# A new order list for an attention and feed-forward kernel: the same 1349 pieces of work, arranged anew

## The chip, the cores and the metric

The kernel runs on one core of a Trainium2 chip. The core's engines work side by side, each through its own queue of instructions, in order: TensorE (PE; PEld for its weight loads), VectorE (DVE), ScalarE (ACT), GpSimd (POOL) and SyncE (SP), which issues most of the DMAs. What is measured is the device time of one execution in microseconds. The kernel before took 220.15 us, the median of three runs (219.94 to 220.78). One execution of it was profiled, and all rows of a profile come from that one.

## The reference

The result is `x + A(xn) + B(xn)` with `xn = layernorm(x)` over 2048 rows of 512 columns.

A is attention with 32 heads of 16 columns over four segments of 512 rows, with a memory that is handed from segment to segment:

```python
p = _softmax(qs @ ks.T * scale + mask)
a_dot = p @ vs
pq, pk = phi(qs), phi(ks)            # phi(t) = t + 1 where t > 0, else exp(t)
a_mem = (pq @ M) / (pq @ z + 1e-06)
o = g * a_mem + (1.0 - g) * a_dot
M = M + pk.T @ vs;  z = z + pk.sum()
```

and then `o @ wo`. B is `silu(xn @ w1) @ w2` with 1792 hidden columns. Weights and x are bf16.

## The kernel before, in words

Rows come in 16 tiles of 128; four tiles are a segment. Nothing is scheduled by a planner at build time: the text `ORDER` (from line 16) lists 1349 words, one for each piece of work, and a loop at the end of the kernel calls the pieces in exactly that order. Each engine gets its instructions in the order in which the words name them, so the list fixes every engine's queue. What words on different engines do in time is settled by the semaphores alone.

A word is a name and its numbers. The ones that matter here:

- `xs`, `xc`+`xd` (statistics of a tile on VectorE, lines 286 and 289), `xq`+`xi` (root on ScalarE and reciprocal, for tiles 0 to 3; `xg` does four tiles on GpSimd for the others), `Nv t` (the norm of tile t on VectorE, line 315).
- `X` (transpose on TensorE, line 845, first segment) with its copies `Xa` on ScalarE and `Xv` on VectorE (line 851); `XD` (transpose by DMA on SP's queue, the later segments).
- `k s.dt.part`, `q`, `v`, `h`: projections, in four parts each for segments 0 and 1 and in two for the others (lines 336 and 338). `kv`, `qv`, `vv` copy the result out of PSUM on VectorE, `ka`, `qa`, `va` on ScalarE (lines 376, 399, 406). `kp` makes the masked keys on GpSimd. `ha` is the tanh on ScalarE (line 492), `hv` the product that completes silu on VectorE (line 497).
- `S n`: a score of 4 heads' blocks, 72 of them, one 4-bank PSUM tile, and behind it the exponential on ScalarE (`Pb`, line 730) and the causal selects on GpSimd (line 744). The list is written with a new line at each `S`; such a line is called a stage.
- `E n`, `O n`: the weighing of the values by the exponentials (line 791), `Ev`, `Ea`, `Ov` their copies out (lines 821, 828). The copies also start small DMAs that gather the softmax sums (`zraw`, line 813). `Om` merges the odd halves.
- `fp`, `fa`, `fv`, `gp`, `ga`, `gv`: phi of the keys and queries; `t` and `m`, `mv`, `mw`: the memory update. `s`, `sv`, `r`, `w`, and in the last segment `R`, `W`: reciprocals of the sums; `z`, `d`: two DMAs each that spread them over the partitions (line 577); `zv`, `dv`, `n`, `nv`: their products and the sum into `oT` (lines 589, 599, 608).
- `o s.j.i`, `oc`, `od`, `oh`: products of the output, whole, half and quarter columns wide. `xl` loads the residual rows, `st` and `sh` add and store.
- `bmask`, `odd`, `omask`, `kind`, `gate`: small constants. `busy` is idle TensorE work at the start.

All results of TensorE but the scores share four PSUM banks (the pool `pp`): a projection, a weighing or an output tile takes a bank with its first product, and the bank is free when the word that copies it out (`kv`, `hv`, `Ev`, `st` and the like) is done. A score needs the score tile free, that is, the exponential of the score before.

A product runs whole (128 x 128 weights) or, between a weighing and the next score, as four column tiles of 32 (`narrow`); the list sets which by what stands ahead of it.

The loads at the start are issued ahead of the list and aren't in it: x tiles 0 and 2 and then wv, wk, wq, x tiles 4 to 7, w1 and the rest of x on SP's queue, x tiles 1 and 3 on ScalarE's.

Of the kernel before, what the change touches and what calls it, by code (L numbers as in the profile page):

```python
# [25 lines left out]
S6 fa0.3 k1.2.0 k1.2.1 k1.2.2 h0.5.0 h0.5.1 h0.5.2 q1.1.0 h0.5.3 ha0.5 k1.2.3 kv1.2 q1.1.1 q1.1.2 hv0.5
S8 h0.7.0 q1.1.3 qv1.1 h0.6.0 h0.6.1 h0.6.2 h0.6.3 ha0.6 fv0.3 E1 Ev1 k1.0.0
S9 hv0.6 h0.7.1 h0.7.2 h0.7.3 Om0 ha0.7 k1.0.1 k1.0.2 kp1.2 q1.0.0 q1.0.1 q1.0.2 fp0.1 Nv9 XD9 xs12 k1.0.3 kv1.0 kp1.0
S10 h0.8.0 hv0.7 h0.8.1 h0.8.2 h0.8.3 ha0.8 h0.9.0 h0.9.1 q1.0.3 t0.3 Nv10 XD10 h0.9.2 h0.9.3 qv1.0
S13 hv0.8 O1 Ov1 xs15 v1.0.0 v1.0.1 v1.0.2 ha0.9 v1.0.3 vv1.0 h0.10.0 h0.10.1 bmask  # L30
S12 k1.1.0 k1.1.1 k1.1.2 t0.2 k1.1.3 kv1.1 h0.10.2 h0.10.3 ha0.10 hv0.9 h1.0.0 Om1 h1.0.1 h1.0.2
S15 h1.10.0 h1.10.1 h1.10.2 hv0.10 kp1.1 xl0.2 h1.0.3 ha1.0 Nv11 XD11 E2 Ev2 O2 Ov2
S17 h1.10.3 k1.3.0 hv1.0 k1.3.1 k1.3.2 k1.3.3 kv1.3 fp1.3 h0.12.0 h0.12.1 xs14 m0.2 mv0.2 ha1.10 h0.12.2
S21 fv0.1 q1.3.0 q1.3.1 q1.3.2 q1.3.3 qv1.3 h1.3.0 hv1.10 gp1.1 h0.12.3 ha0.12 t0.1 h1.3.1 h1.3.2 t0.0 h1.3.3
S14 hv0.12 k2.2.0 h0.11.0 h0.11.1 k2.2.1 h0.11.2 h0.11.3 xl0.0 h0.13.0 ha1.3
S16 ha0.11 h0.13.1 h0.13.2 kp1.3 h0.13.3 xs13 kv2.2 hv1.3 ha0.13 q2.1.0 q2.1.1 qv2.1 E3
S19 Ev3 h1.11.0 h1.11.1 h1.11.2 h1.11.3 hv0.11 O3 hv0.13 fa1.3 k2.1.0 mw0.2 k2.1.1 Ov3 kv2.1 Om2
S24 h1.8.0 h1.8.1 h1.8.2 h1.8.3 m0.0 mv0.0 q2.3.0 q2.3.1 qv2.3 ha1.8 hv1.8
S18 v2.1.0 v2.1.1 vv2.1 ga1.0 k2.0.0 o0.2.7 oc0.2.5.0 ha1.11 sv0 r0.1 o0.2.4 k2.0.1 kv2.0 xg12.4
S22 fv1.3 v2.2.0 v2.2.1 vv2.2 o0.2.1 ga1.1 gp1.2 o0.2.6 o0.0.3 o0.0.13 od0.2.11.1 hv1.11 r0.2 o0.0.10  # L40
S20 o0.2.0 oc0.0.2.0 r0.3 lw1 o0.2.2 od0.0.0.2 oc0.2.10.1 h1.1.0 h1.1.1 h1.1.2 h1.1.3 kp2.1 E4 r0.0 od0.0.0.1 ha1.1 gate w0 gv1.1 kp2.0 z0.1
S28 o0.0.6 hv1.1 z0.2 o0.0.8 z0.3 o0.0.11 o0.0.5 Ev4 oc0.0.7.1 Om3 z0.0 o0.2.8 o0.0.12 ga1.2 O4 Ov4
S26 q2.0.0 q2.0.1 h1.7.0 h1.7.1 h1.7.2 h1.7.3 gv1.2 ha1.7 qv2.0 oc0.2.10.0 od0.0.0.3 oc0.0.2.1
S23 fp1.2 od0.2.11.3 h1.4.0 hv1.7 h1.4.1 h1.4.2 Nv14 o0.2.12 h1.4.3 ha1.4 od0.2.11.0 oc0.0.7.0 zv0.3 h1.9.0 o0.2.13 h1.9.1
S25 h1.9.2 h1.9.3 ha1.9 Nv12 XD12 o0.2.3 oc0.2.5.1 gp1.0 zv0.2 o0.2.16 o0.0.16 hv1.4 zv0.0 XD14 zv0.1 E5 o0.0.17 Ev5 hv1.9
S29 fa1.2 o0.2.17 o0.2.14 k2.3.0 gv1.0 k2.3.1 kv2.3 h1.2.0 h1.2.1 h1.2.2
S27 o0.0.9 mw0.0 O5 o0.2.15 Ov5 o0.2.9 Nv13 fp1.0 XD13 h1.2.3 ha1.2 od0.2.11.2 fv1.2 st0.2 t1.2 o0.0.14 o0.0.15
# [6 lines left out]
S41 o0.1.7 Ev7 o0.3.12 o0.1.1 hv1.5 O7 v2.3.0 mw1.2 fa1.1 Ov7 v2.3.1 vv2.3 fv1.1 t1.1
S37 o0.3.5 q3.3.0 q3.3.1 Om7 qv3.3 od0.1.8.1 s1 o0.1.5 sv1 r1.2 o0.1.10 oc0.1.9.1 st0.1 r1.0 od0.3.3.2 ga2.3 kp2.2
S36 k3.1.0 k3.1.1 q3.1.0 q3.1.1 qv3.1 r1.3 r1.1 w1 d1.2 z1.1 z1.2 ka3.1 o0.3.4
S40 h1.6.0 h1.6.1 h1.6.2 h1.6.3 fp2.3 h2.8.0 h2.8.1 ha1.6 o0.3.7
S43 oc0.3.0.0 o0.3.6 od0.3.3.0 hv1.6 od0.3.3.1 m1.0 mv1.0 oc0.3.2.0 od0.3.3.3 o0.3.15 st0.3 o1.2.8 ha2.8 o1.2.7 hv2.8 fv2.0 E8 Ev8 gp2.3
S38 o1.2.13 fa2.2 v3.0.0 v3.0.1 Om6 k3.0.0 od1.2.1.1 k3.0.1
# [6 lines left out]
S46 oc1.0.10.1 gv2.1 h2.12.0 z1.0 o1.0.5 h2.12.1 O9 Ov9 o1.0.8 ha2.12 hv2.12 t2.3
S49 o1.0.9 o1.0.17 h2.5.0 h2.5.1 kp3.0 ha2.5 n1.1 nv1.1 o1.2.17 fp2.1 oc1.0.10.0 o1.0.12
S53 o1.0.2 hv2.5 oc1.0.7.0 fa2.1 v3.1.0 v3.1.1 vv3.1 o1.0.15 xl2.0 E10 Ev10
S51 o1.2.12 n1.0 od1.0.1.2 xl1.3 od1.2.1.0 h2.4.0 zv1.0 h2.4.1 nv1.0 kp3.1 ha2.4 fv2.1 t2.1 gp2.0 o1.2.15 o1.0.3 hv2.4 o1.0.11
S50 o1.2.14 o1.2.16 st1.2 Om9 O10 Ov10 od1.0.1.1 h2.2.0 h2.2.1 ha2.2 hv2.2 o1.0.14 o1.1.9 od1.1.6.0  # L70
S52 Om10 o1.3.8 oc1.3.3.0 od1.1.6.3 o1.1.2 od1.0.1.0 st1.0 o1.1.15 od1.3.9.1 h2.9.0 h2.9.1 ha2.9 o1.3.15 hv2.9 gv2.2
S56 k3.3.0 k3.3.1 kv3.3 ga2.0 o1.1.17 oc1.1.7.0 xl1.1 E11 Ev11 oc1.3.3.1 oc1.1.10.1 gv2.0
S61 o1.3.7 o1.3.2 ga3.0 o1.1.16 O11 o1.1.13 m2.0 oc1.1.10.0 o1.1.11 o1.3.17 Ov11 od1.3.9.2
S54 mv2.0 od1.1.6.2 m2.2 o1.1.4 mv2.2 mw2.2 s2 sv2 o1.3.5 r2.3 Om11 fill h2.10.0 h2.10.1 ha2.10 hv2.10 gp3.0 o1.3.14
S55 o1.1.12 gv3.0 r2.1 r2.0 o1.3.6 oc1.1.7.1 o1.1.14 o1.3.13 r2.2 w2 o1.3.16 d2.0 h2.13.0 h2.13.1 ga3.1 o1.1.0 ha2.13 hv2.13
S58 h2.3.0 h2.3.1 o1.3.1 o1.1.5 o1.1.8 o1.3.12 od1.3.9.0 o1.3.0 ha2.3 hv2.3
# [866 lines left out]
```

## Time and profile before

| | before |
|---|---|
| median of three runs | 220.15 us |
| the profiled execution | 219.96 us |
| its span, first to last instruction | 218.2 us |
| TensorE busy | 210.9 us (97%) |
| ScalarE busy | 184.1 us (84%) |
| VectorE busy | 181.3 us (83%) |
| GpSimd busy | 127.4 us (58%) |
| exponentials (line 730) | 72, mean 1.878 us |

The profiled execution's 219.96 us is its span and 1.76 us around it. A row of a timeline gives the start in us from the span's beginning, the duration, the engine, the line of the program, the operation, what it writes and reads, a count, and in brackets how long the engine had been idle and for what. Matmuls overlap, so a row's duration is longer than the distance to the next one.

### The profile page before, as it was taken

The page shows a single profiled execution, that of the slowest core. Times are in us where ns is not written, and L with a number is a line of the kernel's source. Part 1 is how long each engine was busy: PE and PEld are TensorE (multiplying, and loading weights), DVE is VectorE, ACT ScalarE, POOL GpSimd, SP SyncE. Part 2 cuts the span into 40 slices and gives each one's busy share as a digit, 9 for nine tenths or more (in the row PEclk, how much of TensorE's full clock was granted, in tenths as well). Part 3 has the DMA queues.
Part 4 walks back from the last instruction along what each step waited for, and adds up shares of the span by engine and source line. Part 5 has one row for each costly group of instructions (what it writes and reads, how often), then busy time and mean ns, then how long its engine had stood idle before and what let it go on. Part 6 is the DMA issues. An engine that isn't in the chain of part 4 may idle for free.

```text
span 218.2 us, 9267 instructions
## 1 busy us (share of the span) xinstructions
PE 210.9 (97%) x3982; PEld 116.1 (53%) x4006; DVE 181.3 (83%) x370; ACT 184.1 (84%) x173; POOL 127.4 (58%) x203
## 2 busy tenths in 40 slices
...
DMA packets 33273, 19.60 MB, mean 90 GB/s; under 512 B 14672, under 2 KB 33232, under 8 KB 33232
## 3 DMA queue, kind: packets, MB, share of 16 engines
...
q14 instruction: 10, 0.08, 0.1%
HBM read 9.96 MB, written 2.10 MB: 55 GB/s over the span
## 4 chain that ended last, share of the span: by engine, by line
PE 92%; DMA 3%; ACT 2%; issue 1%; SPq 1%; DVE 0%
PE ps L336 26%; PE psO L338 17%; PE ps L338 16%; PE psS L724 11%; PE psO L336 9%; PE psV L791 8%; PE psS L338 4%; DMA wk_sb<-in_A_wk_dram 3%; ACT Pb L730 2%; PE psM L452 1%; SPq L169 0%; SPq L158 0%; PE ps L509 0%; ACT th L492 0%; DVE o_half L668 0%
## 5 line engine op out<-in xcount | busy, mean ns | idle before, releaser
L730 ACT ACTIVATE Pb<-psS 128x2048 bf16<-128x2048 f32 x72 | 135.2, 1878 | 4.7 <-PE psS L724 2.4
L744 POOL TENSOR_SCALAR_AFFINE_SELECT Pb<-Pb 128x512 bf16<-128x512 bf16 (+2 forms) x88 | 62.3, 718 | 22.4 <-ACT Pb L730 19.6
L497 DVE SCALAR_TENSOR_TENSOR hT<-th,ps 128x512 bf16<-128x512 bf16 x56 | 38.0, 682 | 10.1 <-ACT th L492 9.4
L744 POOL TENSOR_SCALAR_AFFINE_SELECT lows<-Pb 64x512 bf16<-64x512 bf16 (+1 forms) x40 | 24.3, 607 | 32.0 <-ACT Pb L730 24.9
L338 PE MATMUL psO<-w_sb,hT 128*32 128x512 bf16 (+2 forms) x696 | 41.4, 321 | 0.0
L336 PE MATMUL ps<-xnT,w_sb 128*128 128x512 bf16 (+1 forms) x177 | 35.9, 330 | 0.2 <-issue 0.2
L492 ACT ACTIVATE th<-ps 128x512 bf16<-128x512 f32 x56 | 33.0, 594 | 3.5 <-PE ps L338 3.1
L338 PEld LDWEIGHTS <-hT 128*32 128x32 bf16 x864 | 21.5, 96 | 14.6 <-issue 3.1
L338 PE MATMUL ps<-xnT,w_sb 128*32 128x512 bf16 (+1 forms) x408 | 24.8, 349 | 0.0
L724 PE MATMUL psS<-qT,k 32*128 32x64 bf16 (+3 forms) x512 | 23.0, 233 | 0.2
L336 PEld LDWEIGHTS <-w_sb 128*128 128x128 bf16 x178 | 16.4, 98 | 11.9 <-issue 1.2
L336 PE MATMUL psO<-w_sb,hT 128*128 128x512 bf16 (+2 forms) x82 | 20.5, 324 | 0.7 <-issue 0.6
L791 PEld LDWEIGHTS <-Vz 128*32 128x32 bf16 x768 | 16.1, 97 | 9.5 <-issue 0.6
L791 PE MATMUL psV<-Pb,Vz 128*32 128x448 bf16 (+7 forms) x512 | 21.0, 286 | 0.0
L724 PEld LDWEIGHTS <-k 32*128 32x128 bf16 x512 | 9.3, 92 | 21.2 <-issue 20.4
L336 PE MATMUL ps<-xnT,wk_sb 128*128 128x256 bf16 (+1 forms) x63 | 14.4, 326 | 0.4 <-DMA wk_sb<-in_A_wk_dram 0.2
L724 PE MATMUL psS<-qT,kT 16*128 16x448 bf16 (+3 forms) x256 | 14.7, 269 | 0.0
L338 PEld LDWEIGHTS <-w_sb 128*32 128x32 bf16 x408 | 10.3, 96 | 6.7 <-issue 1.7
L621 DVE SCALAR_TENSOR_TENSOR o_out<-psO,x_res 128x512 bf16<-128x512 f32 x14 | 9.4, 679 | 5.0 <-PE psO L338 3.9
L336 PEld LDWEIGHTS <-hT 128*128 128x128 bf16 x92 | 8.5, 98 | 9.6 <-issue 2.1
L828 DVE CAST odd<-psV 128x512 bf16<-128x512 f32 x16 | 11.0, 687 | 2.4 <-PE psV L791 2.4
L338 PE MATMUL psO<-wo_sb,oT 128*32 128x512 bf16 x140 | 12.8, 379 | 0.0
...
## 6 DMA issues: line engine op xcount, KB each, us to landing
...
```

The source lines that it names most:

```text
L336: return [nc.tensor.matmul(out, lhsT=lhsT, rhs=rhs, start=start, stop=stop, skip_group_check=True)]
L338: nc.tensor.matmul(out[c : c + 32], lhsT=lhsT[:, c : c + 32], rhs=rhs, start=start, stop=stop, tile_position=(0, c), skip_group_check=True,)
L452: nc.tensor.matmul(psM[32 * g : 32 * g + 32, i, :].rearrange("p (r d) -> p r d", d=DH), lhsT=st["phiK", dt][:, j, 32 * g : 32 * g + 32], r ...
L492: nc.scalar.activation(out=th[:], in_=sts[s]["h", ft][:, :], func=AF.Tanh, scale=0.5)
L497: nc.vector.scalar_tensor_tensor(out=st["hT"][:, ft, :], in0=st.pop(("th", ft))[:], scalar=1.0, in1=st.pop(("h", ft))[:, :], op0=ALU.add, ...
L621: out = nc.vector.scalar_tensor_tensor(out=o_out[:], in0=st.pop(("psO", j)), scalar=0.5, in1=st["x", j][:], op0=ALU.mult, op1=ALU.add)
L724: nc.tensor.matmul(psS[:, g, c : c + q2 - q1], lhsT=keys[rows], rhs=st["qT"][rows, dt, q1:q2], start=True, stop=True, tile_position=(32 * ...
L730: exp = nc.scalar.activation(out=blocks(Pb, b).rearrange("p y g c -> p g y c"), in_=psS[:, :, :].rearrange("p g (y c) -> p g y c", c=BLOCK ...
L744: over[id(Pb)].append(nc.gpsimd.affine_select(out=out, in_=in_, compare_op=ALU.is_ge, fill=0.0, base=base, pattern=[[0, out.shape[1]], [1, ...
L791: nc.tensor.matmul(psV[32 * g : 32 * g + 32, q0 : q0 + nq].rearrange("p (y c) -> p y c", y=weights.shape[2]), lhsT=Vzs[s % 2][:, kt, 4 * d ...
L828: copy(out=odd[:], in_=sts[s].pop(("psV", 1))[:, :])
```

## The change

Only the text `ORDER` is replaced. Both lists hold 1349 words. They are the same words but for seven copies that change engine: `ka0.1`, `ka3.1`, `va3.3`, `Ea14` and `Ea15` (ScalarE) become `kv0.1`, `kv3.1`, `vv3.3`, `Ev14` and `Ev15` (VectorE), and `kv0.2` and `Ev10` (VectorE) become `ka0.2` and `Ea10` (ScalarE). The scores stand in the same order in both. In the lines before S0, tile 3's statistics and norm stand ahead of tile 2's, and tile 0's V products ahead of tile 1's transposes.

The lines up to S4, line S11, and the last line (S71, broken here into pieces; after its middle the rest is left out):

```diff
-ones0 ones1 zeros xc0 xd0 xc1 xq0 xi0 Nv0 busy44 xd1 xq1 xc2 busy6 xi1 X0.1 xd2 xq2 Nv1 X1.1 Xa0.1 v0.0.0 v0.0.1 v0.0.2 xs3 xi2 Nv2 xq3 xi3 v0.0.3 X2.1 Xa1.1 k0.1.0 tb Nv3 X3.1 Xv2.1 k0.1.1 Xv3.1 vv0.0 odd omask k0.0.0 k0.0.1 k0.0.2 k0.0.3 ka0.0 fp0.0 q0.0.0 kf0.0 q0.0.1 q0.0.2 q0.0.3 k0.1.2 k0.1.3 q0.2.0 v0.2.0 qa0.0 xs5 ka0.1 kp0.1
-S0 v0.1.0 v0.1.1 xs6 xs7 q0.2.1 v0.2.1 v0.2.2 v0.2.3 vv0.2 fa0.0 k0.2.0 k0.2.1 k0.2.2 xs4 xg4.4
-S2 q0.2.2 q0.2.3 qv0.2 k0.2.3 kv0.2 fp0.2 fa0.2 v0.1.2 v0.1.3 vv0.1 Nv5 Nv6 XD6 q0.1.0 q0.1.1 q0.1.2 q0.1.3 qv0.1
-S1 h0.0.0 h0.0.1 h0.0.2 xs10 h0.0.3 v0.3.0 v0.3.1 v0.3.2 v0.3.3 ha0.0 vv0.3 q0.3.0 kp0.2 hv0.0
-S3 h0.3.0 h0.3.1 q0.3.1 q0.3.2 h0.3.2 tanh XD5 h0.3.3 k0.3.0 Nv7 XD7 q0.3.3 qv0.3 k0.3.1 xs8 ha0.3
-S4 Nv4 h0.1.0 k0.3.2 h0.1.1 hv0.3 XD4 h0.2.0 h0.2.1 h0.2.2 h0.2.3 ha0.2 xs9 k0.3.3 kv0.3 hv0.2
+ones0 ones1 zeros xc0 xd0 xc1 xq0 xi0 Nv0 busy44 xd1 xq1 xc2 X0.1 busy6 xs3 xd2 xi1 Nv1 Xa0.1 v0.0.0 xq3 v0.0.1 v0.0.2 X1.1 xi3 xq2 xi2 Xa1.1 v0.0.3 Nv3 X3.1 Nv2 Xv3.1 X2.1 Xv2.1 tb k0.0.0 k0.0.1 k0.1.0 k0.0.2 k0.0.3 vv0.0 k0.1.1 q0.0.0 q0.0.1 q0.0.2 odd ka0.0 q0.0.3 kf0.0 k0.1.2 fp0.0 qa0.0 xs4 k0.1.3 kv0.1 kp0.1 q0.2.0 fa0.0 bmask
+S0 k0.2.0 xs6 k0.2.1 k0.2.2 k0.2.3 v0.2.0 ka0.2 v0.1.0 v0.2.1 v0.2.2 v0.2.3 xs5 xs7 xg4.4
+S2 v0.1.1 v0.1.2 v0.1.3 vv0.2 q0.2.1 q0.2.2 fa0.2 q0.1.0 q0.1.1 vv0.1 q0.1.2 q0.1.3 qv0.1
+S1 Nv5 XD5 q0.2.3 v0.3.0 v0.3.1 h0.0.0 h0.0.1 h0.0.2 h0.0.3 Nv6 Nv7 XD6 qv0.2 v0.3.2 q0.3.0 XD7 ha0.0 hv0.0 xs11
+S3 h0.3.0 h0.3.1 v0.3.3 vv0.3 Nv4 h0.3.2 XD4 q0.3.1 q0.3.2 h0.3.3 ha0.3 q0.3.3 h0.2.0
+S4 k0.3.0 hv0.3 qv0.3 k0.3.1 h0.2.1 h0.2.2 h0.2.3 ha0.2 h0.1.0 h0.1.1 k0.3.2 k0.3.3 xs9 kp0.2 kv0.3 fp0.3
...
-S11 hv0.4 q1.2.0 q1.2.1 q1.2.2 v1.3.1 kind fa0.1 q1.2.3 qv1.2 v1.3.2 v1.3.3 vv1.3 Nv8 XD8 O0 lw0 kp0.3 fv0.0 Ov0
+S11 hv0.4 q1.2.2 v1.1.3 q1.2.3 qv1.2 fa0.3 vv1.1 O0 omask Nv11 v1.3.0 v1.3.1 Ov0 v1.3.2 fp0.2 fv0.3
...
-S71 o2.3.11 o2.3.0 o2.3.17 o2.1.8 h3.13.0 h3.13.1 ha3.13 hv3.13 o2.3.15 R0.2 o2.3.1 oh11.0 oh5.0 o2.1.1 od2.1.9.3 dv3.3 oh11.1 xl2.1 oh7.1 oh9.0 E15 O15 Ea15 Ov15
...
+S71 o2.3.17 hv3.3 o2.3.6 oc2.3.5.1 h3.6.0 h3.6.1 ha3.6 o2.3.1 o2.1.10 h3.13.0 h3.13.1 oc2.3.5.0 oh4.0 o3.2.0 R0.0 o2.3.14 R0.3 oh11.1 od2.1.9.0 d3.1 o3.2.12 hv3.6 oh1.0 E15 R0.1 oc2.1.3.0 o2.1.17 o3.2.5 o3.2.10 ha3.13 hv3.13 d3.0 oh5.1 oh6.0 O15 o2.1.11 Ev15 dv3.1 o3.0.5 oc3.0.12.1 od3.0.3.1 o3.0.6 dv3.3 od3.0.3.2 o2.3.11 Ov15
...
+W1 z3.2 oc2.1.0.0 st2.1 o3.1.2 o3.2.13 oh2.1 o3.1.3 o3.0.13 zv3.0 o3.1.1 n3.0 nv3.0 o2.3.3 o3.0.4 o2.3.9 z3.3
...
+n3.3 o3.2.15 oc3.1.10.1 oh10.0 o3.2.8 oh15.1 oh3.0 oc3.1.10.0 o3.1.15 o3.2.9 o3.0.15 nv3.3 o3.0.17
```

The other 65 stages, and the rest of S71, are rearranged in the same way; most words stay in their stage or move by a few.

More of the change, by code (lines that the diff above doesn't have):

```diff
@@ L26 @@
[L26 to L47, printed above, removed]
```

110 lines of the change are left out of this document (66 added, 44 removed).

## The prediction

> **What bounds the kernel now.** I read the page's totals first, then the busy time by stretch, then the chain that ended last, then the engines' own timelines at the start, where the list is changed most.
>
> ```profile
> span 218.2 us, 9267 instructions
> PE 210.9 (97%) x3982; PEld 116.1 (53%) x4006; DVE 181.3 (83%) x370; ACT 184.1 (84%) x173; POOL 127.4 (58%) x203
> ...
> PE 92%; DMA 3%; ACT 2%; issue 1%; SPq 1%; DVE 0%
> ```
>
> TensorE carries 92% of the chain. The stretches (start:end, length, then busy time of PE, PEld, DVE, ACT, POOL) say how close the others are behind it:
>
> ```profile
> 12.40:60.00 47.60, 47.08 (x848) 28.66 (x857) 45.09 (x95) 46.98 (x42) 35.78 (x57) 1.00 0.48 124
> 120.00:190.44 70.44, 69.30 (x1317) 35.06 (x1326) 58.57 (x114) 66.70 (x61) 42.59 (x66) 1.00 0.23 62
> 190.44:218.20 27.76, 24.82 (x620) 15.22 (x612) 17.52 (x34) 4.21 (x5) 0.86 (x3) 1.00 0.24 72
> ```
>
> From the first exponential (12.40) to 60 us VectorE is busy 45.1 of 47.6 us and ScalarE 47.0, so three engines are full there; after 120 us VectorE has a sixth of its time free. The granted clock is 1.00 throughout. So a new list can save little: the products are the same ones, and their price is fixed by these rows.
>
> ```profile
> 2.68 5.81 DMA wk_sb<-in_A_wk_dram
> 8.54 0.39 PE ps L336 x2
> ...
> 19.21 0.36 PE psS L724 x8
> ...
> 101.68 0.86 PE ps L338 x16
> ...
> 115.73 0.86 PE ps L336 x4
> ...
> 193.47 1.10 PE psV L791 x48
> ...
> 214.38 0.90 PE psS L338 x32
> ```
>
> Four products in whole tiling (x4) take 0.86 us, and so do four in column tiling (x16), so one is 0.215; a score is 0.36, a pair of weighings (E and O) 1.10. The dense work starts when wk lands (2.68 + 5.81 = 8.49) and ends at 214.38 + 0.90 = 215.28; the last store and its landing fill the rest of the span. The ScalarE timeline gives the beat:
>
> ```profile
> 9.53 0.20 ACT L309 ACTIVATE spare<-eps 128x1 f32<-128x1 f32 x1
> 10.30 0.58 ACT L376 CAST kT<-ps 128x512 bf16<-128x512 f32 x1 [0.58 <-PE ps L336]
> ...
> 12.40 1.88 ACT L730 ACTIVATE Pb<-psS 128x2048 bf16<-128x2048 f32 x1
> ...
> 17.20 1.88 ACT L730 ACTIVATE Pb<-psS 128x2048 bf16<-128x2048 f32 x1
> ...
> 19.59 1.88 ACT L730 ACTIVATE Pb<-psS 128x2048 bf16<-128x2048 f32 x1
> ...
> 22.01 1.88 ACT L730 ACTIVATE Pb<-psS 128x2048 bf16<-128x2048 f32 x1
> ...
> 24.38 1.88 ACT L730 ACTIVATE Pb<-psS 128x2048 bf16<-128x2048 f32 x1
> ```
>
> A usual stage is one score and nine products: 0.36 + 9 x 0.215 = 2.29 us, and it lasts 19.59 - 17.20 = 2.39 us; 0.10 us goes at each score, where TensorE changes its tiling to rows and back. Stage S4 (22.01 to 24.38) holds eight products, 2.08 + 0.10, but lasts 2.37 us: that is ScalarE's floor, one exponential and one short operation.
>
> **The change, part by part.** The list is a new arrangement of the same 1349 words, except that seven evacuations change engine: k0.1, k3.1, v3.3, E14 and E15 go from ScalarE to VectorE, k0.2 and E10 the other way. Tilings change 144 times in both lists, so 144 x 0.05 us is in both. Twelve word-sized pieces go from column tiling to whole; both cost the same (above), so nothing is put down for them.
>
> *The start.* The VectorE rows of the layernorms:
>
> ```profile
> 6.15 0.38 DVE L315 TENSOR_SCALAR xn_t<-x_lo,mv_all,rstd_all 128x512 bf16<-128x512 bf16 x1
> ...
> 6.45 0.69 DVE L286 BATCH_NORM_STATS2 stats<-x_lo 128x6 f32<-128x512 bf16 x1
> 7.17 0.18 DVE L289 BATCH_NORM_AGGREGATE mv_all<-stats 128x2 f32<-128x6 f32 x1
> 7.27 0.13 DVE L306 RECIPROCAL rstd_all<-rstd_all 128x1 f32<-128x1 f32 x1
> ```
>
> Tile 3's statistics take 7.27 - 6.45 = 0.82 us and now stand ahead of tile 1's norm, which slips from 6.15 to about 7.0. That hurts nobody: V of tile 0 no longer waits behind tile 1's transposes, and no k product can run before 8.49. Norms, transposes and copies of tiles 3 and 2 then follow by about 9.25, just when the second k column half wants them (8.6 + 3 x 0.215 = 9.25). Before, k0.1.0, tile 3's transposes and k0.1.1 stood ahead of k0.0; now one half-pair does. So k0.0 is complete near 9.7, and ScalarE, free after its table load and first exponential (9.73; some 0.3 later now, since tile 1's copies come 0.3 later), copies it at 10.0 instead of 10.30. Behind it the same chain of copies follows (fa0.0 takes the place of ka0.1), and the first exponential starts 0.30 earlier, at 12.1. Bounds: 0.0, if tile 3's x or wq lands later than its first reader in the old order showed, and 0.45, if ScalarE alone sets it. Price: -0.30.
>
> *One product less is done by then.* 21 product-sized words stand ahead of S0, 22 before: +0.21. It comes back in S4, which gets nine products instead of eight and thereby uses the 0.19 us that the floor wasted: -0.19. S11 becomes short (six products, one weighing and the score, 2.19 + 0.10) and meets the floor of 2.37: +0.08.
>
> *VectorE's queue in S0 to S3.*
>
> ```profile
> 11.51 0.69 DVE L286 BATCH_NORM_STATS2 stats<-x_hi 128x6 f32<-128x512 bf16 x1 [0.23 <-DMA x_hi<-in_A_x_dram]
> ...
> 16.53 0.68 DVE L406 CAST Vz<-ps 128x512 bf16<-128x512 f32 x1
> 17.13 1.18 DVE L315 TENSOR_SCALAR xn_t<-x_hi,mv_all,rstd_all 128x512 bf16<-128x512 bf16 x2
> 18.22 0.68 DVE L399 CAST qT<-ps 128x512 bf16<-128x512 f32 x1
> ...
> 20.80 0.41 DVE L315 TENSOR_SCALAR xn_t<-x_hi,mv_all,rstd_all 128x512 bf16<-128x512 bf16 x1
> ...
> 22.86 0.38 DVE L315 TENSOR_SCALAR xn_t<-x_hi,mv_all,rstd_all 128x512 bf16<-128x512 bf16 x1
> 23.16 0.68 DVE L497 SCALAR_TENSOR_TENSOR hT<-th,ps 128x512 bf16<-128x512 bf16 x1
> ```
>
> ```profile
> 19.48 0.61 PE L336 MATMUL ps<-xnT,w_sb 128*128 128x256 bf16 x4
> ```
>
> x of tiles 4 to 7 lands at 11.5 whatever the list says, and the new list puts xs4 there too, ahead of kv0.1. From 11.51 on its queue is: xs4, kv0.1, bmask (moved here from S13), xs6, xs5, xs7, vv0.2, vv0.1, qv0.1, Nv5, Nv6, Nv7, qv0.2. Four statistics at 0.82, five copies from PSUM (kv0.1, bmask as one of them) at 17.13 - 16.53 = 0.60, and three norms at 0.30 to 0.55 (23.16 - 22.86, and half of 18.22 - 17.13) put qv0.2's start at 11.51 + 3.28 + 3.0 + 0.9 to 1.65 = 18.7 to 19.4, its end 0.7 later: 19.4 to 20.1. Its bank is what h0.3.0 needs in S3: q0.2, v0.3, h0.0 and q0.3 hold all four banks of the rotation. S0's score starts at 12.1 less its 0.36 and a tenth for the hand-over, and by the beat S3 starts at 11.65 + 3 x 2.39 = 18.8 and h0.3.0 is due at 19.25. TensorE waits 0.2 to 0.9 us there; everything else on it is queued behind h0.3.0, the scores included. Before, the same word found a bank free (qT's copy at 18.22 was over at 18.9 and h0.3.0, the last row, came at 19.48). Which end is nearer depends on what GpSimd does at the time:
>
> ```profile
> 17.53 0.63 POOL L417 TENSOR_SCALAR pos<-kT 128x512 bf16<-128x512 bf16 x1
> ...
> 19.94 1.09 POOL L744 TENSOR_SCALAR_AFFINE_SELECT Pb<-Pb 128x1024 bf16<-128x1024 bf16 x1
> ```
>
> The slow second norm of 17.13 ran beside pos (17.53 to 18.16); the one at 20.80 ran in 0.41 us inside a select (19.94 to 21.03). In the new list GpSimd has only selects and the root around S1, so I take the short end: +0.30. The Trainium skill (SBUF — State Buffer, "Who interferes with whom") has it that a VectorE tensor_scalar in a 2-port mode and any GpSimd instruction exclude each other for the whole instruction. The trace agrees for pos, not for the select at 19.94; by the rule each norm would be held behind a select and the wait would come to the long end, +0.9, a sum of 220.8 in place of 220.2.
>
> *The other bank waits.* By the list, 20 of 175 bank takings come within 0.5 us of product work of the word that frees them, 16 before; three of the closest new ones (k1.3.0 on Ev2 in S15, m2.0 on Ov11 in S61, o0.0.5 on hv1.11 in S18) leave 0 to 0.3 us when VectorE's casts are laid 0.60 apart. Bounds 0 and +0.5; I take +0.1, near zero, as the old list shows no such wait at all.
>
> *Engine moves.* Three casts more on VectorE (1.8 us) lie at the start (costed above), in S40 to S42 and in the tail, where it is busy 17.5 of 27.8 us: hidden. Ea10 keeps ScalarE until 0.2 us past the next score; the 2.6 us of products in S51 cover it. The loads of w2 and wo, the layernorm transposes of tiles 4 to 15 and the phi transposes keep at least two stages to their readers: nothing.
>
> *The tail.* 24.0 us of products stand after S71, 24.9 before, so 0.85 us of them fills earlier stages; the total is unchanged. But O15 stands 18.3 us of work from the end instead of 21.0, and the last product that needs its sums (o3.0.17) 4.2 instead of 5.4. From the end of O15 the chain now has 13.55 us where it had 15.1. Its links:
>
> ```profile
> 195.85 1.05 SPq L813 DMA_DIRECT2D zraw<-odd  x2
> ...
> 197.95 7.32 SPq L577 DMA_DIRECT2D spr<-rz  x8
> ...
> 198.83 0.55 DVE L560 RECIPROCAL ri<-zraw 32x64 f32<-32x64 bf16 x1
> ...
> 207.40 0.41 DVE L589 TENSOR_TENSOR oT<-spr,oraw 128x512 bf16<-128x512 bf16 x1
> ...
> 208.32 0.69 DVE L608 TENSOR_TENSOR oT<-ps,oT 128x512 bf16<-128x512 f32 x1 [0.50 <-PE ps L338]
> ```
>
> VectorE first has Ev15, dv3.1 and dv3.3 (1.4), then Ov15 0.7, two issues of sums 1.05, landing at most 1.9 (196.90 to 198.83), four reciprocals 2.1, the weighting 0.35, st2.1 and its store ahead of z3.3 on SP's queue (1.1), z3.3's two issues 1.35, landing at most 2.1 (205.27 to 207.40), its product 0.4 and the sum 0.7: 13.1 of 13.55. Hidden, by 0.4. The residual loads of S71 keep 1 us to their stores, and the last half store has the same end as before.
>
> **Sum**, against the profiled execution (219.96 us: span 218.2 and 1.76 around it; 0.2 under the median of 220.15): -0.30 + 0.21 - 0.19 + 0.08 + 0.30 + 0.10 = +0.20, 220.16, given as 220.2 us.
>
> **Rivals.** *The tail chain comes out late (slower).* Before, the same chain took 14.44 us, from the end of O15 (193.47 + 1.10) to the end of the last sum (209.01). That holds waits which nobody minded, which speaks against it; for it speaks that the new list puts Ev15 and a store into it. At 14.44, o3.0.17 stalls 0.9 us: 221.1. From 14.7 on it passes half a per cent. *The norms are slow and h0.3.0 waits 0.9 us*: 220.8; for it the row at 17.13, against it the one at 20.80. *No new wait at all*: 220.16 - 0.40 = 219.8; for it the old list's lack of any bank wait, against it the queue counted above. *The reordered start does nothing*, since wk's landing hides it or tile 3's x comes late: +0.30, with the bank wait smaller by as much, so 220.2 to 220.5.
>
> **How the numbers follow.** Forecast, the case of the idle start in it, 219.9 to 220.6: 0.53. No new wait: 0.14. Slow norms: 0.10. Late tail: 0.15, most of it past 221.2. More bank waits than I found: 0.08, past 221.2. Range 219.5 to 221.4; the likeliest case's own is 219.9 to 220.6. Half a per cent (1.1 us) is about what a measurement can tell from no change. Faster by that needs more than all gains counted: 0.04. Slower, from late tail and bank waits: 0.21. Same: 0.75.
>
> **What would show it.** First exponential at 12.1; a wait of TensorE for VectorE's qT copy before the first tanh product of S3, at 19.2; S4 at 2.39 or more; no other wait of TensorE for VectorE over 0.2 us; the last products unbroken to the end. I am wrong if the first exponential isn't earlier, if S3 runs through, or if TensorE waits in the last 15 us.

## The result, and the profile after

| | before | changed |
|---|---|---|
| median (six runs each) | 220.17 us | 222.94 us |
| lowest to highest | 219.94 to 221.09 | 222.44 to 223.51 |
| profiled execution | 219.96 us | 223.51 us |
| its span | 218.2 us | 221.8 us |

The change makes the kernel slower: ratio 1.0116, 95% interval 1.0098 to 1.0135. The medians differ by 2.77 us. The forecast was 220.2 us, with a range of 219.5 to 221.4. The profiled execution of the changed kernel happens to be the slowest of its six.

The page of the changed kernel, totals and chain (engine shares):

```profile
span 221.8 us, 9176 instructions
...
PE 212.1 (96%) x3938; PEld 115.8 (52%) x3964; DVE 182.2 (82%) x373; ACT 183.3 (83%) x170; POOL 126.8 (57%) x203
...
PE   8899999989999999999999999999989999999993
...
PE 75%; DVE 6%; ACT 6%; DMA 5%; POOL 4%; issue 2%; SPq 1%; POOLq 0%
```

The busy times have hardly changed, but TensorE now carries 75% of the chain instead of 92%: VectorE, ScalarE, GpSimd and DMAs have come between its products. TensorE's row stands for the span in 40 slices of 5.5 us, and behind the start its eights mark two places, at 44 to 50 us and at 161 to 166. TensorE's waits, summed by what released it (engine, line, total, times, longest), name these two and a third:

```profile
PE ps L336 <- DVE oraw L821: 0.7, 1, 0.7
PE psV L791 <- POOL pos L417: 0.6, 1, 0.6
PE ps L338 <- DVE Vz L406: 0.4, 1, 0.4
PE ps L336 <- issue: 0.3, 2, 0.2
PE ps L336 <- DMA wk_sb<-in_A_wk_dram: 0.3, 1, 0.3
```

The second line is a wait for kT's copy, as the row of the weight load below shows; the view puts it down to `pos`, which ended at about the same time and which the waiting product doesn't read. The same view of the kernel before has only one wait for work on a bank, 0.2 us for line 468, and the changed kernel has that one too. To see what each costs, I take the start of each exponential less the products that the list puts ahead of it (at the prediction's prices), for both kernels; the difference is the time lost up to that stage. In the profiled pair it is:

| up to the exponential of | lost so far, us | what came in |
|---|---|---|
| S0 | 0.55 | start |
| S7 | 0.37 | S4's floor gave 0.18 back |
| S6 | 0.44 | S11 met the floor |
| S13 | 1.24 | the first wait (S8 to S10) |
| S17 | 1.87 | the second wait (S15) |
| S59 | 2.11 | small waits |
| S60 | 2.92 | the third wait (S59) |
| TensorE's last product | 2.94 | |

Another 0.6 us lies behind the last product, where SP finishes issuing the last store 1.43 us after TensorE's end instead of 0.83. Together 3.5 us, which is the difference of the two profiled executions.

*The start.* Rows of the changed kernel:

```profile
9.07 1.21 PEld L336 LDWEIGHTS <-wk_sb 128*128 128x128 bf16 x12 [0.43 <-DMA wk_sb<-in_A_wk_dram]
10.57 0.77 PEld L336 LDWEIGHTS <-wq_sb 128*128 128x128 bf16 x8 [0.30 <-DMA wq_sb<-in_A_wq_dram]
...
12.06 0.69 DVE L286 BATCH_NORM_STATS2 stats<-x_hi 128x6 f32<-128x512 bf16 x1 [0.71 <-DMA x_hi<-in_A_x_dram]
```

All loads land half a microsecond later than in the profile before (wk then 8.49, x_hi 11.51), so the first exponential starts at 12.74, not at 12.1.

*The first wait.*

```profile
31.01 1.03 POOL L300 TENSOR_TENSOR rstd_all<-rstd_all,expo 128x4 f32<-128x4 f32 x1
32.01 0.66 POOL L744 TENSOR_SCALAR_AFFINE_SELECT Pb<-Pb 128x512 bf16<-128x512 bf16 x1
...
32.08 0.74 DVE L315 TENSOR_SCALAR xn_t<-x_hi,mv_all,rstd_all 128x512 bf16<-128x512 bf16 x1 [0.45 <-POOL rstd_all L300]
...
33.91 0.66 POOL L744 TENSOR_SCALAR_AFFINE_SELECT lows<-Pb 64x512 bf16<-64x512 bf16 x1 [0.63 <-ACT Pb L730]
33.94 1.16 DVE L433 SCALAR_TENSOR_TENSOR pk<-ex,pos 128x512 bf16<-128x512 bf16 x1
...
35.04 0.68 DVE L406 CAST Vz<-ps 128x512 bf16<-128x512 f32 x1
...
35.77 1.05 PE L338 MATMUL ps<-xnT,wk_sb 128*32 128x512 bf16 x16 [0.41 <-DVE Vz L406]
...
37.74 1.88 ACT L730 ACTIVATE Pb<-psS 128x2048 bf16<-128x2048 f32 x1 [0.91 <-PE psS L724]
```

The norm of tile 11 (`Nv11`) was moved from S15 to S11, where its root on GpSimd isn't ready. It waits 0.45 us at the head of VectorE's queue; the copy `Ov0`, two sums of phi (line 433) and V's copy `vv1.3` stand behind it. Two of these operations also last longer beside GpSimd's selects: the norm 0.74 us (0.38 to 0.41 alone), and the second sum 1.16 us (the one before it 0.68). `k1.0.0` needs the bank that `vv1.3` frees; and all of TensorE stands behind `k1.0.0`, the next score included.

*The second wait.*

```profile
46.52 1.09 POOL L744 TENSOR_SCALAR_AFFINE_SELECT Pb<-Pb 128x1024 bf16<-128x1024 bf16 x1
...
46.98 0.64 DVE L245 TENSOR_TENSOR evec<-evec,evec 128x1 f32<-128x1 f32 x1
...
47.61 0.67 DVE L376 CAST kT<-ps 128x512 bf16<-128x512 f32 x1
...
48.34 0.50 PEld L791 LDWEIGHTS <-Vz 128*32 128x32 bf16 x16 [0.80 <-DVE kT L376]
...
50.87 1.88 ACT L730 ACTIVATE Pb<-psS 128x2048 bf16<-128x2048 f32 x1 [0.50 <-PE psS L724]
```

The five small operations of `kind` were moved from S11 to S12, ahead of kT's copy `kv1.1`. The fourth of them, one element per partition, takes 0.64 us and ends with GpSimd's select (46.98 + 0.64 = 47.62, 46.52 + 1.09 = 47.61). In the kernel before, with GpSimd idle, it took 0.16:

```profile
30.64 0.16 DVE L245 TENSOR_TENSOR evec<-evec,evec 128x1 f32<-128x1 f32 x1
```

E2 then waits for `kv1.1`'s bank. How much of the loss the 0.48 us of that one operation make, apart from the place of all five, wasn't measured.

*The third wait.*

```profile
159.64 3.62 SPq L577 DMA_DIRECT2D spr<-rz  x4
...
164.34 0.42 DVE L599 TENSOR_TENSOR phiQT<-spr,phiQT 128x512 bf16<-128x512 bf16 x1 [1.87 <-DMA spr<-rz]
...
164.69 0.68 DVE L821 CAST oraw<-psV 128x512 bf16<-128x512 f32 x1
...
165.42 1.02 PE L336 MATMUL ps<-xnT,w_sb 128*128 128x512 bf16 x4 [0.66 <-DVE oraw L821]
```

`dv2.0` was moved from S60 to S57, ahead of the copy `Ev12`; it waits 1.87 us for the spread DMAs of `d2.0`, and `h3.7.0` waits for `Ev12`'s bank.

All three have one shape: a VectorE word that is held up by another engine or by a DMA now stands ahead of a copy that frees one of the four banks.

### The profile page after: what moved, and what is told of

It reads as the page before. It is cut to its first block, busy times and chain, and to the rows that moved or that the text cites. A ratio compares the mean times of both kernels' runs of the same rounds, so it can differ in the third digit from the quotient of the medians.

```text
span 221.8 us, 9176 instructions
## 1 busy us (share of the span) xinstructions
PE 212.1 (96%) x3938; PEld 115.8 (52%) x3964; DVE 182.2 (82%) x373; ACT 183.3 (83%) x170; POOL 126.8 (57%) x203
## 4 chain that ended last, share of the span: by engine, by line
PE 75%; DVE 6%; ACT 6%; DMA 5%; POOL 4%; issue 2%; SPq 1%; POOLq 0%
PE ps L336 16%; PE psO L338 15%; PE ps L338 14%; PE psO L336 9%; PE psS L724 8%; PE psV L791 7%; ACT Pb L730 5%; PE psS L338 4%; DMA wk_sb<-in_A_wk_dram 3%; DMA spr<-rz 2%; DVE hT L497 1%; POOL Pb L744 1%; ACT th L492 1%; POOL lows L744 1%; DVE stats L286 1%
## 5 line engine op out<-in xcount | busy, mean ns | idle before, releaser
L744 POOL TENSOR_SCALAR_AFFINE_SELECT lows<-Pb 64x512 bf16<-64x512 bf16 (+1 forms) x40 | 23.2, 580 | 36.1 <-ACT Pb L730 30.7
L338 PE MATMUL psO<-w_sb,hT 128*32 128x512 bf16 (+2 forms) x612 | 39.2, 326 | 0.0
L336 PE MATMUL ps<-xnT,w_sb 128*128 128x256 bf16 (+1 forms) x177 | 35.1, 320 | 1.2 <-DVE oraw L821 0.7
L338 PEld LDWEIGHTS <-hT 128*32 128x32 bf16 x780 | 19.1, 97 | 12.8 <-issue 3.0
L336 PE MATMUL psO<-w_sb,hT 128*128 128x512 bf16 (+2 forms) x107 | 24.9, 318 | 0.8 <-issue 0.6
L791 PE MATMUL psV<-Pb,Vz 128*32 128x320 bf16 (+7 forms) x512 | 21.4, 286 | 0.6 <-POOL pos L417 0.6
L336 PEld LDWEIGHTS <-hT 128*128 128x128 bf16 x113 | 10.1, 98 | 11.3 <-issue 1.9
L338 PE MATMUL psO<-wo_sb,oT 128*32 128x512 bf16 x148 | 13.6, 380 | 0.0
L385 POOL TENSOR_SCALAR k<-kT,pm_odd 128x512 bf16<-128x512 bf16 x15 | 11.1, 740 | 2.7 <-DVE kT L376 1.8
L417 POOL TENSOR_SCALAR pos<-kT 128x512 bf16<-128x512 bf16 x12 | 8.2, 684 | 7.0 <-ACT kT L376 6.8
```

Source lines behind the costliest of these rows:

```text
L336: return [nc.tensor.matmul(out, lhsT=lhsT, rhs=rhs, start=start, stop=stop, skip_group_check=True)]
L338: nc.tensor.matmul(out[c : c + 32], lhsT=lhsT[:, c : c + 32], rhs=rhs, start=start, stop=stop, tile_position=(0, c), skip_group_check=True,)
L385: nc.gpsimd.tensor_scalar(out=to, in0=frm, scalar1=keep[:, 0:1], scalar2=1.0, op0=ALU.mult, op1=ALU.mult)
L417: nc.gpsimd.tensor_scalar(out=pos[:], in0=phi_src(s, of, dt), scalar1=3.0e38, scalar2=0.0, op0=ALU.min, op1=ALU.max)
L744: over[id(Pb)].append(nc.gpsimd.affine_select(out=out, in_=in_, compare_op=ALU.is_ge, fill=0.0, base=base, pattern=[[0, out.shape[1]], [1, ...
L791: nc.tensor.matmul(psV[32 * g : 32 * g + 32, q0 : q0 + nq].rearrange("p (y c) -> p y c", y=weights.shape[2]), lhsT=Vzs[s % 2][:, kt, 4 * d ...
```

## The experiments

Each kernel was timed in alternation with the kernel before. Medians in us, ratios to the kernel before with 95% intervals:

| run | what it is | median | ratio |
|---|---|---|---|
| n11 | changed, Nv11 back | 222.96 | 1.0127 (1.0103 to 1.0150) |
| kind | changed, kind later | 221.98 | 1.0076 (1.0048 to 1.0104) |
| dv20 | changed, dv2.0 back | 222.27 | 1.0091 (1.0068 to 1.0113) |
| three | these three | 222.24 | 1.0091 (1.0068 to 1.0113) |
| four | three, and w2's load back | 221.71 | 1.0063 (1.0041 to 1.0085) |
| om1 | three, and Om1 back | 222.61 | 1.0108 (1.0085 to 1.0130) |
| root | changed, root earlier | 223.31 | 1.0136 (1.0111 to 1.0160) |
| five | four, Om2 back, old order of the end | 221.46 | 1.0053 (1.0032 to 1.0074) |
| six | four, Om2 back, a third order of the end | 220.92 | 1.0018 (0.9997 to 1.0040) |
| tail | changed, old order of the end | 223.26 | 1.0124 (1.0096 to 1.0151) |
| tail2 | changed, third order of the end | 222.81 | 1.0093 (1.0061 to 1.0124) |
| oldhead | changed, old head | 223.48 | 1.0149 (1.0125 to 1.0174) |
| newhead | before, new head | 220.73 | 1.0026 (1.0005 to 1.0048) |
| newhead2 | the same, kind later | 220.53 | 0.9999 (0.9982 to 1.0017) |

The runs fall into four sessions, in which the kernel before had medians of 220.41 (n11, kind, dv20, three), 220.39 (four, om1, root, oldhead), 220.17 (five, tail, newhead) and 220.45 us (six, tail2, newhead2), and 220.17 beside the changed kernel above. Across sessions the ratios are the safer comparison.

### The three waits, one by one

```diff
-S11 ... O0 omask Nv11 v1.3.0 v1.3.1 Ov0 ...        (n11, three)
+S11 ... O0 omask v1.3.0 v1.3.1 Ov0 ...
-S12 ... ha0.10 kind XD11 k1.1.0 ... kv1.1 ...      (kind moved in kind, three)
+S12 ... ha0.10 k1.1.0 ... kv1.1 ...
+S15 ... h1.0.3 Nv11 XD11 O2 Ev2 Ov2 ...
+S14 ... kv2.2 kind
-S57 ... fill dv2.0 d2.3 E12 Ev12 ...               (dv20, three)
+S60 ... hv3.7 dv2.0 zv2.0 ...
```

> The changed kernel with one move: tile 11's norm (Nv11) and its transpose go back from S11 and S12 to S15. Theory (a wait at the head of VectorE's queue): at 32.08 this norm waits 0.45 us for GpSimd's root, V's copy behind it frees its bank late, and k1.0.0 and the next exponentials lose 0.87 us. Without it the median falls from 222.9 by 0.7 to 0.9, to about 222.1; the wait of 0.41 at k1.0.0 is gone, and S8 lasts 2.7 where it lasted 3.30. Rival A (VectorE is simply full up to 44 us, so that whatever is taken out lets the next wait come up): under 0.3 us gained, 222.6 to 222.9, with a wait of TensorE for VectorE of the same size within the next three stages. Rival B (the time is lost at the start and the tail, the stages between only pass it on): 222.9.

> The changed kernel with one move: the five small operations of kind go from S12 to the end of S14, where VectorE has the least to do. Theory: their third operation (0.64 us beside GpSimd's select, 0.16 before) delays kT's copy kv1.1, and E2 waits 0.57 us for its bank; moved away, S15 lasts 2.45 instead of 3.05 and the median is 0.6 lower, about 222.3. Rival A (VectorE is full, the delay moves on): under 0.2 us gained. Rival B (start and tail): 222.9.

> The changed kernel with one move: the product dv2.0 goes from S57, ahead of the copy Ev12, to S60, behind hv3.7. Theory: at 164.34 it waits 1.87 us for the spread transfer, Ev12 stands behind it, and h3.7.0 waits 0.66 us for Ev12's bank; S59 and S60 lose about 0.8 together. Moved, S59 lasts 2.8 instead of 3.59 and the median is 0.8 lower, about 222.1. Rival A (the transfer is late for what follows as well): n2.0 or its sum waits instead, under 0.3 us gained. Rival B (start and tail): 222.9.

> The three moves together (Nv11 with XD11 to S15, kind to S14, dv2.0 to S60). Theory: the gains add, 0.9 + 0.6 + 0.8 = 2.3 of the 2.77 lost: about 220.6, ratio to the kernel before 1.002; no wait of TensorE for VectorE over 0.3 us is left. Rival A (VectorE full up to 44 us): only the third move counts, about 222.0. Rival B (start and tail): 222.5 or more.

`kind` gave 0.96 and `dv20` 0.67 by the medians (0.9 and 0.55 by the ratios), where 0.6 and 0.8 were expected. `n11` gave nothing and `three` only 0.70 of the 2.3: the gains did not add. In the profile of `three`, S8's loss was gone as expected (0.95 lost at S6, 0.98 at S9), but 0.97 came in between S12 and S15, at a place that had cost nothing:

```profile
39.50 1.07 SPq L813 DMA_DIRECT2D zraw<-oraw  x2
...
40.62 1.19 SPq L441 DMA_TRANSPOSE phiK<-pk  x1
...
45.84 0.52 DVE L835 COPY_PREDICATED oraw<-omask,odd 128x256 int32<-128x256 int32 x1 [1.59 <-DMA zraw<-oraw]
...
46.98 0.38 PE L336 MATMUL ps<-xnT,w_sb 128*128 128x512 bf16 x1 [0.43 <-DVE Vz L406]
```

`Om1` overwrites `oraw` and must wait until the sums have left it. Their DMA, issued at 39.50, lets go of it only at 45.8, and V's copy stands behind `Om1`. `n11` has the same: `Om1` waits 1.33 us at 44.77, and 0.97 comes in between S12 and S15 where S8's loss has gone. In the changed kernel S8's wait, which comes behind the issue of w2's load, had put the sums and `Om1` off by so much that this one stayed hidden. It is a fourth wait of the same shape, and the change made it too: `Om1` went from S12 to S13, ahead of `vv1.0`.

The third wait is not there in every execution. Seven profiles have `dv2.0` in S57. In n11, kind and oldhead it started 2.9 us after the first of its spread issues and S59 lost nothing; in the changed kernel, root, tail and tail2 4.7 to 5.1 us after, with waits of TensorE of 0.66 to 1.26 and a loss of 0.8 to 1.4. SP's issues of that line differ likewise (shortest, median and longest in ns, first and last start); of the changed kernel and of `kind`:

```profile
L577 SPq DMA_DIRECT2D spr<-rz x6: 602/620/1570, 159.6 to 163.9; - x6
```

```profile
L577 SPq DMA_DIRECT2D spr<-rz x8: 602/604/656, 158.1 to 163.2; - x8
```

In all four late ones, and in `three`, one of these six issues took 1.17 to 1.89 us, the fourth or the fifth and not `d2.0`'s own two; in the early ones none over 0.66. So the move of `dv2.0` made the kernel depend on a transfer that comes 2 us late in some executions. Such long issues aren't made by the change: the kernel before has two of line 577, 1.10 and 1.41 us at 110.8 and 118.4. In the traces of all sixteen profiles, each of the 39 issues of that line over 0.7 us overlaps a 16 KB packet of the DMA queue that the page calls "instruction" (q8); but so do 183 of the 857 shorter ones, those of `n11`, `kind` and `oldhead` at this place among them. What decides between the two isn't known.

### The wait behind the wait

```diff
-S6 ... vv1.3 kp0.3 lw0 q1.1.0 ...                  (four: three, and)
+S11 ... O0 lw0 omask ...
-S13 O1 Ov1 v1.0.0 Om1 fp0.1 ...                    (om1: three, and)
+S12 ... kv1.1 kp1.1 h1.0.0 Om1 h1.10.1
```

> The three moves of the run before, and the load of w2 (lw0) back from S6 to S11, behind O0. In the three-move kernel the stages up to S13 lost only 0.0 against the kernel before, but the merge Om1 then waited 1.59 us at 45.84 for the sums that leave oraw (issued at 39.50), V's copy behind it was late, and S13 and S12 lost 0.97. Theory (the w2 load of some 8 us, started later, runs beside the layernorm transposes on SP's queue, and the sums queue behind them): with the load back at its old place the sums land early, Om1 does not wait, about 1.0 us less than the three moves alone, 221.2 to 221.4. Rival A (Om1 stands too early whatever the load does): a wait of over 1 us at Om1 stays, 222.2. Rival B (the time is lost at the start): 222.2 and no wait.

> The three moves, and the merge Om1 moved back from S13 to S12, behind kT's copy kv1.1 (where the kernel before has it); the w2 load stays in S6. Theory: V's copy vv1.0 no longer stands behind Om1's wait, so S13 and S12 run at 2.4 and the median is about 1.0 lower than with the three moves alone, 221.2 to 221.4; Om1 itself waits not at all or where nobody queues for it. Rival (the sums are so late that the wait moves to what now stands behind Om1, h1.0's tanh product): under 0.3 gained, 222.0 or more.

`four` shows that w2's load holds the sums. The change had moved w2's load (1.8 MB) from S11 to S6. By stretches (the last two columns are the DMA engines' busy share and GB/s), the changed kernel still moves 314 and 247 GB/s between 34 and 42 us, where the kernel before was nearly done:

```profile
34.00:38.00 4.00, 3.59 (x69) 1.83 (x69) 4.00 (x10) 2.92 (x4) 3.83 (x6) 1.00 0.96 314
38.00:42.00 4.00, 3.84 (x46) 2.86 (x45) 3.44 (x6) 3.99 (x4) 1.23 (x3) 1.00 1.42 247
```

```profile
34.00:38.00 4.00, 3.95 (x89) 2.63 (x90) 3.90 (x9) 3.85 (x5) 2.22 (x4) 1.00 0.97 215
38.00:42.00 4.00, 4.00 (x66) 2.50 (x68) 3.80 (x9) 3.92 (x5) 2.81 (x5) 1.00 0.34 69
```

(first the changed kernel, then the kernel before). In that time the layernorm transposes and the sums go through SP's queue. In the five profiles with the load in S6 in which `Om1` waits for the sums (n11, three, root, tail, tail2) it starts 11.8 to 12.4 us behind the issue of the load, but 5.0 to 6.3 us behind that of the sums. With the load issued at 29.65 again, `Om1` starts at 43.70 without a wait, S12 loses nothing (0.44 lost at S12, 0.44 at S15), and the median falls by 0.53. Part of the expected 1.0 went to a fifth wait, `Om2`, which the change had moved from S19 to S17, ahead of M's copy `mv0.2`:

```profile
51.91 0.57 DVE L835 COPY_PREDICATED oraw<-omask,odd 128x256 int32<-128x256 int32 x1 [0.99 <-DMA zraw<-oraw]
...
52.38 0.21 DVE L464 COPY M<-psM 128x64 f32<-128x64 f32 x1
...
52.65 0.38 PE L336 MATMUL ps<-xnT,w_sb 128*128 128x256 bf16 x2 [0.28 <-DVE M L464]
```

It costs 0.45 between S21 and S14, where `three` lost 0.14. In `om1`, the load left late, the merge moved: S13 and S12 ran clean, but VectorE, with `Om1` and two norms between `kv1.1` and `Ev2`, was late for S15 (0.57); `Om2` (0.45) and a wait in S41 (0.32) followed. That is the rival's outcome.

```diff
-S7 ... xs8 ...   S5 ... xs10 xg8.4 ...             (root)
+S4 ... xs9 xs10 xs8 xg8.4 ...
```

> The changed kernel with the two last statistics of tiles 8 to 11 (xs10, xs8) and GpSimd's root xg8.4 moved up into S4, so that tile 11's norm in S11 finds its root done; the norm itself stays where the change put it. Theory (the wait, not the norm's own 0.4 us of work, makes the bank late): the 0.45 wait at Nv11 goes, S8 and S9 together lose 0.3 or less instead of 0.7, and the median is 0.4 to 0.8 lower, 222.1 to 222.5. Rival (VectorE has too much work ahead of V's copy vv1.3 in any case): S8 still lasts 3.1 or more, 222.9.

With the root done early, `Nv11` in S11 starts at 31.82 without a wait and S8 lasts 37.28 - 34.57 = 2.71 us instead of 3.30, with the norm where the change put it. So with the norm in the same place, and lasting 0.72 us there, the bank came in time: the wait made it late, and with it the second sum of phi, which now ran clear of the select in 0.68 us instead of 1.16. The median did not show it: the two statistics, now ahead of `kv0.3`, made E0 wait 0.56 at 26.29, `Om1`'s wait came up as in `three` (0.97), and this execution had the late spread (1.4).

### The end

> All that was found: Nv11 and XD11 in S15, kind in S14, dv2.0 in S60, the w2 load behind O0 in S11, the merge Om2 from S17 to S19 behind kv2.1, and the last words in the old order. The last but the kernel with the first four moves had one wait of TensorE over 0.2 us left, 0.28 at 52.65 for M's copy behind Om2, and S21 lost 0.45 there. Theory (the loss is the sum of these places, nothing is spread over the rest): 221.7 less 0.45 and less 0.4 to 0.8, that is 220.4 to 220.9, the ratio to the kernel before 1.000 to 1.002. Rival (the list is tight everywhere, so that a new wait comes up where one goes): 221.4 or more.

> The changed kernel with the words behind o3.0.17, the last 7 us, put into the order that the old list gives them; nothing else is moved. In nine profiles of the new ending (the changed kernel and the runs so far) SP finishes issuing the last half store 1.04 to 1.87 us after TensorE's last product, in the old list 0.83: three stores of 128 KB leave shortly ahead of the two half stores, which then take 0.87 to 1.55 together instead of 0.33 each. Theory (the new order of the last stores costs 0.2 to 1.0): 0.4 to 0.8 off the median, 222.2 to 222.5, and the last issue ends about 0.8 behind the last product. Rival (the end is set by the products, a late issue is within what runs differ by): under 0.2 off, 222.7 to 223.1.

> The kernel with all the moves found (Nv11 and XD11 in S15, kind in S14, dv2.0 in S60, the w2 load in S11, Om2 in S19), with another order of the last words: the products of st3.2 first, then those of st3.1, of the first half store, of st3.0, and of the second half store, so that the five outputs are ready 0.6 to 1.0 us apart. With the old list's order of these words TensorE ended level with the kernel before (-0.07 by work done), but the last issue stood 2.07 us behind TensorE's end (0.83 before), since two stores became ready only at 214.16 and three more queued on VectorE behind them. Theory (the rest of the loss is that bunching): the last issue ends 0.8 to 1.0 behind TensorE's end, 1.1 less than 221.46, that is 220.3 to 220.5. Rival (the landings of the last stores, not their order, make the end): 221.2 or more.

> The changed kernel with that order of its last words and nothing else moved. Theory (the change's own ending bunches its stores: 216.20, three of them, then two half stores that take 1.55 together, the last issue 1.43 behind TensorE's end): 0.4 to 0.7 off the 222.94, 222.2 to 222.6. Rival: under 0.2 off.

```diff
-S17 ... kv1.3 kp1.3 Om2 kp1.2 ... mv0.2            (five, six)
+S19 ... kv2.1 Om2 xs12 ...
-... o3.2.7 st3.2 o3.1.14 oh4.1 ... st3.1 ... st3.0 ... sh0 ... sh1   (six, tail2)
+... o3.2.7 st3.2 o3.1.17 ... st3.1 oh16.0 ... sh0 o3.0.10 ... st3.0 oh4.1 ... sh1
```

In `five` TensorE ends level with the kernel before (-0.07 us by product work), and in `six` the chain is TensorE's again and no wait of TensorE for a copy over 0.2 us is left (its page's chain, then TensorE's waits; the 1.1 is at the start, in the kernel before too):

```profile
PE 94%; DMA 1%; issue 1%; DVE 1%; SPq 0%; DVEq 0%
```

```profile
PE psO L336 <- issue: 1.1, 7, 0.2
PE psS L864 <- DVE zraw L188: 1.1, 1, 1.1
PE ps L336 <- issue: 0.3, 2, 0.2
PE psO L336 <- DVE hT L497: 0.2, 1, 0.2
```

So in `five`'s profile nothing is left of what the change lost before TensorE's last product, with six words moved back (`Nv11` with `XD11`, `kind`, `dv2.0`, `lw0`, `Om2`) and all others ahead of the last 7 us left where the change put them. (`six` has 0.44 there, 0.26 of it from its start and 0.25 between S41 and S37.) `six` stands 0.18% over the kernel before, with an interval that includes no difference. For the ending itself the test was poor. My first order (`five`, `tail`) let all outputs become ready in the last 3 us, and the last issue ended 2.07 us behind TensorE; the third order (`six`, `tail2`) brought 1.53 and 1.03, against 1.43 in the changed kernel and 0.83 before. `tail` came out at 1.0124, no better than the change's 1.0116, the rival's outcome. `six` gained 0.54 on `five` by the medians and 0.8 by the ratios, where 1.1 was expected. `tail2` gained 0.13 on the changed kernel by the medians, which is the rival's outcome, but 0.5 by the ratios (1.0093 against 1.0116), which is the theory's; the intervals overlap, so it is open. That the change's ending costs anything isn't shown.

### The head

```diff
+ones0 ... S4 of the old list, then the new list from S7      (oldhead)
+ones0 ... S4 of the new list, then the old list from S7      (newhead)
-S11 ... v1.3.1 kind fa0.1 ...                               (newhead2: newhead, and)
+S16 ... kv2.2 kind hv1.3 ...
```

Some words stand elsewhere in the two lists' first stages, and each must come once. So `oldhead` also has `xs11` in S7, `fp0.3` in S5 and `bmask` in S13, and `newhead` also has `xs8` in S7, `xs10` and GpSimd's root `xg8.4` in S5 and `omask` in S11: neither is a change of the head alone.

> The changed kernel with the old list up to the end of S4 (tile 2's norm ahead of tile 3's, tile 1's transposes ahead of tile 0's V, bmask in S13 again), and the new list behind it. In the new head's five profiles the first exponential started between 12.12 and 13.25, each time 3.7 us behind wk's landing or 2.17 behind wq's; the old head's one profile has 12.40 with wk at 8.49. Theory (the landings move the start by half a microsecond from run to run, the two heads are within 0.2 us of each other): 222.7 to 223.3, that is -0.2 to +0.4 against the changed kernel. Rival (the new head costs what the change lost): the median falls by 0.5 or more, to 222.4 or less.

> The kernel before with the new list's head and stages up to S4 (tile 3's norm ahead of tile 2's, tile 0's V ahead of tile 1's transposes, bmask and kv0.1 early) and its own list behind it. The changed kernel with the old head came out at 223.48, 0.54 over the changed kernel. Theory (the new head gains 0.2 to 0.3 where the loads land alike, as the first exponential stands 3.67 behind wk's landing in the new list and 3.91 in the old): 219.9 to 220.2, ratio 0.998 to 1.000. Rival (the new head's VectorE order costs time in the stages behind it, as the changed kernel is slower from S8 on): 220.7 or more.

> The kernel before with the new head (as run before: 220.73), and kind moved out of S11 into S16. In that run TensorE waited 0.51 us at 34.86 for the copy Ov0 in a stretch in which VectorE was not idle for a moment, and S6 lost 0.84. Theory (S11 has no slack on VectorE, so 0.6 us of small operations taken out there comes back in full): 0.6 to 0.8 lower, 219.9 to 220.1, the gain of the new head (0.2) at last seen. Rival (the wait comes from the norm Nv8 behind GpSimd's root, not from the load): 220.6 or more.

The old head made the changed kernel 0.54 slower, not faster, and its profile loses at the same places from S6 on (1.14 by S13, 0.69 from S12 to S17), without the late spread at S59. So the head isn't where the time went. In the old list the new head came out 0.56 slower, through one wait for the copy `Ov0`, in a stretch where VectorE was never idle:

```profile
33.24 0.14 DVE L235 CAST omask<-pm_odd 128x1 int32<-128x1 f32 x1
33.29 0.90 DVE L433 SCALAR_TENSOR_TENSOR pk<-ex,pos 128x512 bf16<-128x512 bf16 x1
...
34.12 0.68 DVE L828 CAST odd<-psV 128x512 bf16<-128x512 f32 x1
...
34.86 0.40 PE L338 MATMUL ps<-xnT,w_sb 128*32 128x256 bf16 x8 [0.51 <-DVE odd L828]
```

With `kind` out of that stage the wait is gone, S6 and S8 together lose 0.29 instead of 0.73, and the kernel equals the kernel before; the gain of 0.2 that I expected on top isn't seen. In the profiled execution a late spread cost 0.76 in S64 (TensorE waited 0.58 for the sum into `oT`), and 0.72 were lost in S64 in `newhead`'s; whether that holds back the median isn't known.

## Why the prediction was wrong

It named the cause as a rival ("more bank waits than I found", 8%) and gave it too little. Step by step:

- **The other bank waits (+0.10, bounds 0 and 0.5): the step that failed.** In place of +0.10 it measured 0.80 (S8 to S13) + 0.63 (S15) + 0.81 (S59) = 2.24 us in the profiled execution. I had looked for bank takings that follow the word that frees them closely in product work and laid VectorE's casts 0.60 apart. The three that struck were none of the three I named (k1.3.0, m2.0, o0.0.5), since the delay doesn't come from the freeing word's distance but from what stands ahead of it in VectorE's queue: a norm that waits for GpSimd, a small operation that takes 0.64, a product that waits for a DMA. I walked that queue for S0 to S3 only.
- **Loads and transposes "keep two stages to their readers: nothing".** True of the readers of w2, wrong for its neighbours: the load, later by about 3.8 us, met the transposes and sums on SP's side. Hidden in the changed kernel, it costs 1 us as soon as the first wait is taken away.
- **The start (-0.30, bounds 0.0 and -0.45).** In the profiled execution it came out 0.34 later than before, past the bound, since the weights landed later. In fourteen profiles with the new head the first exponential starts at 12.10 to 13.25, the middle ones at 12.29 and 12.37; the old head's two have 12.40 and 12.39. Where the weights landed early it was the predicted 12.1 (`kind` 12.12). From TensorE's first product on wq the fourteen took 2.17 to 2.27 us, the old head's two 2.37 and 2.40, so the head itself is worth 0.1 to 0.2. In medians no gain shows (`newhead` 1.0026, `newhead2` 0.9999).
- **One product less (+0.21, -0.19, +0.08).** Held: the loss fell by 0.18 at S4 (2.41 us long) and rose by 0.07 at S11.
- **h0.3.0's wait in S3 (+0.30).** It did not come: S1 to S4 run at 2.39 to 2.41 us, TensorE ran through. VectorE was done with `qv0.2` at 19.50, before `h0.3.0` came up at 19.82. The mis-sized term is `bmask`, which I counted as a copy of 0.60: it kept VectorE 0.13 us (13.46 to 13.59). The three norms took the short end that I chose (17.79 to 18.82).
- **The Trainium skill's rule** (SBUF — State Buffer, "Who interferes with whom") bore on a second place besides the norms: it says that a VectorE instruction with two inputs in SBUF contends with a GpSimd instruction that reads SBUF. The trace agrees at the second wait: line 245 adds two SBUF operands, took 0.64 us beside a select, and ended with it. It doesn't in `newhead`, where the same line took its usual 0.16 us at 31.21 beside GpSimd's root (30.74 to 31.76), which reads SBUF too. For the norms the prediction read the trace wrongly: it took the norm of 20.80 (0.41 us, inside a select) to speak against the rule. That select had only 0.22 us left. In the sixteen profiles 83 norms began while a select or a GpSimd operation of line 417 or 385 still had 0.27 us or more to run, and every one of them ended 0.14 to 0.15 us behind it. So selects do hold norms; in S1 of the changed kernel that came to 0.06 us for one norm of three (17.79), as the select was nearly over.
- **The tail.** The chain of the last sums held: TensorE's products ran unbroken to the end. "The last half store has the same end as before" did not in the profile (1.43 against 0.83 us behind TensorE's end); as a price it isn't settled.
